# Seven block products instead of eight: the second MLP's first product by 2x2 blocks

## The chip, the cores and the metric

The kernel runs on one core of a Trainium2 chip. Its time is the device time of one execution in microseconds, from three timed executions; beside them one execution was taken by the hardware profiler, with the start and length of each instruction on the five engines: PE (TensorE matmuls; PEld are its weight loads), DVE (VectorE), ACT (ScalarE), POOL (GpSimd), and SP, whose queue issues the DMAs.

## The reference

Attention over pooled keys and values, followed by two MLPs ("layers" here) on the 4608 x 512 result:

```python
k_p = k.reshape(B, H, Sp, pool, D).mean(axis=3)          # B=8, H=8, S=576, D=64, pool=8
v_p = v.reshape(B, H, Sp, pool, D).mean(axis=3)
attn = softmax(scale * q @ k_p.T)                         # maximum subtracted, sum + 1e-9
x = (attn @ v_p) -> 4608 x 512
h = x @ w_in1;  x1 = (h * sigmoid(h)) @ w_out1            # 512 x 2048, 2048 x 512
h = x1 @ w_in2; out = (h * clip(h + 3, 0, 6) / 6) @ w_out2
```

The weights come as 64-bit floats.

## The kernel before, in words

The tokens are cut into 9 groups of 512, and the 2048 hidden columns into 16 chunks of 128 (`f`). The first layer runs group by group, each through its 16 chunks; then the second layer does the same. Each operand is kept as two float32r halves, high and low, and a product is made of three: high x high, low x high, high x low.

For one chunk, `h_mm` (L426) makes 12 matmuls into a PSUM tile `hps` of 512 tokens: 3 products x 4 pieces of the 512 contracted columns, each with a weight load of 128 columns and 512 moving columns. `act_a` and `act_b` turn it into `gh` and `gl`: ACT applies the activation (L439 tanh in the first layer, L444 relu in the second), DVE multiplies (L440, L445), ACT copies the rounded high half (L453), DVE subtracts for the low half (L454). `y_mm` (L471) then makes 12 matmuls of 512 columns into four PSUM tiles `y0` to `y3` that collect a whole group. PE runs `y_mm` of a chunk behind `h_mm` of the next one. When a group is through, `y_out` evacuates y0 and y2 on ACT (L480), y1 and y3 on DVE (L482), and SP writes them out: to DRAM tiles `x1` in the first layer, to the output in the second.

In the first layer the attention for the next group's four tiles of 128 tokens is put between the chunks (`scores` L286, softmax on DVE and ACT, transposes, `weighted` L390, `split_x` L406 and L407). The keys and values of a batch are pooled beside it: `pool_k` (L217, DVE) and `pool_v` (L227 to L229, POOL). Also beside it the second layer's weights are turned from 64-bit to two float32r halves, in half pieces of 256 columns (`half_a` on ACT and DVE, `half_b` on ACT and POOL, L168 and L169), and written to DRAM tiles `w2`. In the last group of the first layer they are loaded back, two of 512 KB per chunk (`load_split`), and the second layer keeps all of them in SBUF. The second layer's x of each group is loaded from `x1` and split on ACT and POOL (L502, L503).

Each engine executes its instructions in the order in which the program has them; there is no scheduler, the loops set that order, and semaphores make an instruction wait for its operands and for the buffers that it overwrites. PSUM has two buffers for `hps`, two for the attention's `aps`, and the four y tiles. At the start `warm_wide` lets PE work on zeros (L263, L265, L267), before any data has come; L274 to L390 are attention of the first tiles.

The functions that the change touches:

Of the kernel before, what the change touches and what calls it, by code (L numbers as in the profile page):

```python
# [9 lines left out]
F32 = mybir.dt.float32  # L10
# [8 lines left out]
POOL = 8  # L19
# [5 lines left out]
def kernel(  # L25
# [25 lines left out]
    PW = 2 * SP  # L51
    Q = 32
# [6 lines left out]
    p2 = ctx.enter_context(tc.tile_pool(name="p2", bufs=2))  # L59
    dram = ctx.enter_context(tc.tile_pool(name="dram", bufs=1, space=DRAM))  # L60
# [35 lines left out]
    def split_a(layer, f, piece, mul=False):  # L96
# [4 lines left out]
        mag = p2.tile([P, DM], F32, tag="wmag", name="wmag", bufs=4)  # L101
# [31 lines left out]
    HW = DM // 2  # L133
# [4 lines left out]
    def load_half(f, piece, a):  # L138
        raw = p2.tile([P, HW, 2], U32, tag="wmag", name="hraw", bufs=4)
# [4 lines left out]
    def half_a(f, piece, a):  # L144
        raw = half_raw[f, piece, a]
        hw = raw[:, :, 1]
        mag = p2.tile([P, HW], F32, tag="hmag", name="hmag", bufs=1)
# [15 lines left out]
    def half_b(f, piece, a):  # L163

        raw = half_raw.pop((f, piece, a))
        mag = half_mag.pop((f, piece, a))
        t = raw.rearrange("p f w -> p (f w)").rearrange("p (a f) -> p a f", a=2).bitcast(F32R)
        nc.scalar.activation(t[:, 0], mag, AF.Copy)  # L168
        nc.gpsimd.tensor_tensor(out=t[:, 1], in0=mag, in1=t[:, 0].bitcast(F32), op=ALU.subtract)  # L169
        later.append(lambda: nc.sync.dma_start(  # L170
            out=w2[f][piece][:, :, a * HW:(a + 1) * HW], in_=t.bitcast(F32)
        ))

    def load_split(f, piece):
        t = wts.tile([P, 2, DM], F32R, tag=f"{'io'[piece]}{f}", name="whl")
        nc.sync.dma_start(out=t.bitcast(F32), in_=w2[f][piece])
        if piece == 0:
            t = t.rearrange("p a (c f) -> p a c f", f=P)
        w_sl[1, f, piece] = (t[:, 0], t[:, 1])
# [16 lines left out]
    def load_v(b, j, tag=None):  # L196
        if tag:
            t = staging(tag, 2 * POOL * D)[:SP]
        else:
            t = p2.tile([SP, 2 * POOL * D], F32, tag="v", name="vraw", bufs=1)  # L200
# [45 lines left out]
    def load_q(t, tag=None):  # L246
        qt = staging(tag, DM) if tag else p2.tile([P, DM], F32, tag="q", name="qT")
# [517 lines left out]
```

## Time and profile before

| | |
|---|---|
| three timed executions | 1667.47, 1669.53, 1669.57 us; median 1669.53 |
| profiled execution | 1669.22 us, span 1667.4 us |
| PE, busy | 1615.8 us, 97% of the span, 8016 matmuls |
| DVE, ACT, POOL, busy | 49%, 34%, 15% of the span |
| mean granted PE clock | 0.99 |
| first chunk of the second layer starts at | 914.9 us |

A row of the order of time gives start, length, engine, line of the kernel, instruction, what it writes and reads by the program's names, and how many equal ones were merged; in brackets the idle time of the engine before it and who ended that. Matmuls are pipelined: a row of eight lasts from the first one's start to the last one's end, while the next row starts before that end. So PE's pace is read from starts.

### The profile page before, as it was taken

To read this page: it belongs to the slowest core of one execution; us is meant where nothing else is said; L and a number is where in the kernel's file an instruction comes from. 1 tells how busy PE (TensorE), PEld (TensorE's weight loads), DVE (VectorE), ACT (ScalarE), POOL (GpSimd) and SP (SyncE) were. 2 spreads that over 40 slices of the span, in tenths; PEclk is the share of its full clock that TensorE was granted. 3 is DMA by queue.
4 is the path that set the end of the run, shared out by engine and by line. 5 is a ranking of instruction groups with operands and counts; after the bars stand their busy time and mean duration, and the time that the engine had idled before them with its cause. 6 is when DMAs were issued, how large, how long until landed. Compare 5 with 4: busy or idle time off the path is not lost.

```text
span 1667.4 us, 20343 instructions
## 1 busy us (share of the span) xinstructions
PE 1615.8 (97%) x8016; PEld 1395.7 (84%) x8016; DVE 820.8 (49%) x1356; ACT 560.6 (34%) x1007; POOL 255.1 (15%) x258
## 2 busy tenths in 40 slices
PE   7777999999999999999999999999999999999999
PEld 6565888888878888888888888888888888888887
DVE  6999768667676676744422222222222222222222
ACT  5354433334333333322222323232323232222322
POOL 4755413022131120300000000000000000000000
PEclk9799999999999999999999999999999999999999
DMA  9250335345353443311156201010101010101000
GB/s 298 90 201 21 120 124 163 116 128 182 124 157 113 159 146 131 128 45 63 40 198 218 82 7 45 7 44 7 45 7 45 7 44 7 44 7 45 1 26 26
DMA packets 77184, 144.33 MB, mean 87 GB/s; under 512 B 7840, under 2 KB 32288, under 8 KB 77088
## 3 DMA queue, kind: packets, MB, share of 16 engines
q1 hardware_dynamic: 77088, 143.03, 26.0%
q8 instruction: 63, 1.03, 0.3%
q14 instruction: 33, 0.27, 0.1%
HBM read 96.34 MB, written 46.66 MB: 86 GB/s over the span
## 4 chain that ended last, share of the span: by engine, by line
PE 84%; DVE 8%; DMA 4%; issue 2%; ACT 1%; SPq 1%; POOL 0%; DVEq 0%; POOLq 0%; ACTq 0%
PE y L471 41%; PE hps L426 40%; PE aps L390 1%; PE aps L286 1%; DVE wmag L109 1%; DVE wmag L106 1%; DVE gl L454 1%; DVE wmag L116 1%; DVE t L440 1%; DMA wraw<-in_moe_w_out_dram 1%; DMA hraw<-in_moe_w_out_dram 1%; DMA stage<-in_v_dram 1%; DMA stage<-in_q_dram 1%; DMA bl<-bT 0%; DMA wraw<-in_moe_w_in_dram 0%
## 5 line engine op out<-in xcount | busy, mean ns | idle before, releaser
L426 PE MATMUL hps<-xh,whl 128*128 128x512 f32 x2304 | 546.4, 380 | 4.2 <-POOL whl L127 2.1
L426 PEld LDWEIGHTS hps<-xh,whl 128*128 128x128 f32 x2304 | 435.9, 189 | 67.4 <-POOL whl L127 2.5
L471 PE MATMUL y<-gh,whl 128*128 128x512 f32 x1152 | 357.4, 392 | 1.6 <-POOL whl L127 1.2
L471 PE MATMUL y<-whl,gh 128*128 128x512 f32 x1152 | 342.6, 379 | 0.0
L454 DVE TENSOR_TENSOR gl<-t,gh 128x512 fp32r<-128x512 f32 x288 | 221.1, 768 | 190.5 <-ACT gh L453 190.5
L445 DVE SCALAR_TENSOR_TENSOR t<-t,hps 128x512 f32<-128x512 f32 x144 | 99.1, 688 | 436.3 <-ACT t L444 436.3
L426 PE MATMUL hps<-xl,whl 128*128 128x512 f32 x1152 | 296.8, 380 | 1.8 <-DVE xl L407 1.8
L453 ACT ACTIVATE gh<-t 128x512 fp32r<-128x512 f32 x288 | 181.3, 630 | 290.8 <-DVE t L440 181.5
L471 PEld LDWEIGHTS y<-gh,whl 128*128 128x128 f32 x1152 | 217.2, 193 | 39.3 <-issue 3.7
L426 PEld LDWEIGHTS hps<-xl,whl 128*128 128x128 f32 x1152 | 218.1, 190 | 34.0 <-DVE xl L407 3.0
L471 PEld LDWEIGHTS y<-whl,gh 128*128 128x128 f32 x1152 | 217.7, 189 | 30.9
L444 ACT ACTIVATE t<-hps,three 128x512 f32<-128x512 f32 x144 | 99.2, 689 | 422.2 <-PE hps L426 422.2
L471 PE MATMUL y<-gl,whl 128*128 128x512 f32 x576 | 223.4, 388 | 13.5 <-DVE gl L454 13.4
L471 PE MATMUL y<-whl,gl 128*128 128x512 f32 x576 | 218.4, 379 | 0.0
L440 DVE SCALAR_TENSOR_TENSOR t<-t,hps 128x512 f32<-128x512 f32 x144 | 97.8, 679 | 164.6 <-ACT t L439 164.0
L439 ACT ACTIVATE t<-hps 128x512 f32<-128x512 f32 x144 | 85.8, 596 | 260.8 <-PE hps L426 260.6
L503 POOL TENSOR_TENSOR xl<-xr,xh 128x512 fp32r<-128x512 f32 x36 | 45.9, 1274 | 826.4 <-ACT xh L502 826.4
L471 PEld LDWEIGHTS y<-gl,whl 128*128 128x128 f32 x576 | 111.2, 193 | 33.3 <-DVE gl L454 17.1
L471 PEld LDWEIGHTS y<-whl,gl 128*128 128x128 f32 x576 | 108.9, 189 | 15.8 <-DVE gl L454 0.3
L169 POOL TENSOR_TENSOR hraw<-hmag,hraw 128x256 fp32r<-128x256 f32 x64 | 47.0, 734 | 387.5 <-ACT hraw L168 343.3
L127 POOL TENSOR_TENSOR whl<-wmag,whl 128x512 fp32r<-128x512 f32 x32 | 53.2, 1681 | 50.1 <-ACT whl L126 50.0
L310 ACT ACTIVATE pr<-pr 128x288 f32<-128x288 f32 x64 | 28.4, 443 | 85.2 <-DVE pr L303 85.2
(76 smaller groups left out, 929.0 us busy)
## 6 DMA issues: line engine op xcount, KB each, us to landing
w<-hraw SPq DMA_DIRECT2D x64, 256.0 KB
whl<-w SPq DMA_DIRECT2D x32, 512.0 KB
bl<-bT SPq DMA_DIRECT2D x28, 384.0 KB
x<-o SPq DMA_DIRECT2D x36, 256.0 KB
xr<-x SPq DMA_DIRECT2D x36, 256.0 KB
out_dram<-o SPq DMA_DIRECT2D x36, 256.0 KB
wraw<-in_moe_w_in_dram SPq DMA_DIRECT2D x16, 512.0 KB
wraw<-in_moe_w_out_dram SPq DMA_DIRECT2D x16, 512.0 KB
```

The lines of the kernel that those rows point to most:

```text
L127: nc.gpsimd.tensor_tensor(out=t[:, 1, :], in0=mag, in1=t[:, 0, :].bitcast(F32), op=ALU.subtract)
L169: nc.gpsimd.tensor_tensor(out=t[:, 1], in0=mag, in1=t[:, 0].bitcast(F32), op=ALU.subtract)
L310: nc.scalar.activation(p_t[t][:, a], p_t[t][:, a], AF.Exp, scale=ESCALE)
L426: nc.tensor.matmul(ps, w[:, c, :], shuffled(x[:, c, :]), start=(c == 0 and n == 0), stop=(c == NKC - 1 and n == 2),)
L439: nc.scalar.activation(t2, h, AF.Tanh, scale=0.5)
L440: nc.vector.scalar_tensor_tensor(out=t2, in0=t2, scalar=1.0, in1=h, op0=ALU.add, op1=ALU.mult)
L444: nc.scalar.activation(t2, h, AF.Relu, bias=three)
L445: nc.vector.scalar_tensor_tensor(out=t2, in0=t2, scalar=6.0, in1=h, op0=ALU.min, op1=ALU.mult)
L453: nc.scalar.activation(gh, t, AF.Copy)
L454: nc.vector.tensor_tensor(out=gl, in0=t, in1=gh.bitcast(F32), op=ALU.subtract)
L471: nc.tensor.matmul(ps, a, shuffled(b), start=(f == 0 and n == 0), stop=(f == NF - 1 and n == 2))
L503: nc.gpsimd.tensor_tensor(out=xl[:, c, :], in0=r, in1=xh[:, c, :].bitcast(F32), op=ALU.subtract)
```

## The change

The second layer's first product, 512 tokens x 512 by 512 x 512 for a round of four chunks (`d` = 0 to 3), is taken as a 2x2 by 2x2 product of blocks of 256, in seven block products (Winograd's form of Strassen's scheme) instead of eight. It takes seven combined blocks of the weights per round (`ws`) and seven combined blocks of x per group (`x_st`), and sums of the products afterwards.

- *Weights.* In groups 1 to 7 of the first layer `pair_jobs` takes two chunks' half pieces, adds and subtracts them on POOL (`combine`), splits each of the seven results into high and low and writes it to `ws`. The second product's weights go to `w2` as before. The steps are spread over 12 of 16 chunks (`SPLITTING`), so that the 81 steps fill nearly seven groups, where 64 filled a good five before.
- *SBUF.* Attention's tiles lie in a pool `att` that is closed before the last group of the first layer; the second layer's new tiles (`late`) take its place. Three of the seven factors per round stay in SBUF (`STAYING`), the other four (`PASSING`) have one buffer each and are loaded again for every round.
- *Operands of x.* `make_x` makes the seven blocks of a group from the four loaded blocks of `x1`: four differences and seven subtracts for the low halves on POOL, seven copies on ACT. For the next group this is done in rounds 2 and 3 of a group, between the halves.
- *A round.* PE makes product 0, 5, a y, 4, 6, a y, 3, 1, a y, 2, a y; the y are those of the round before. Each product is 12 matmuls of 256 columns. A copy on ACT (L878) and seven sums on DVE (L862) make the four quarters u4, u3, c1, u2 of h; `act_half` activates each: relu (L612), multiply (L613, both operands in SBUF), copy (L620), subtract (L621).
- *Keys and values.* They are loaded at every fourth chunk instead of every second and pooled two chunks later, and the buffers of `kraw` go from two to one; the transposed probabilities `bT` share a buffer with `vraw`.

The diff, cut to its core:

```diff
-    def half_b(f, piece, a):
-        raw = half_raw.pop((f, piece, a))
-        mag = half_mag.pop((f, piece, a))
-        t = raw.rearrange("p f w -> p (f w)").rearrange("p (a f) -> p a f", a=2).bitcast(F32R)
+    def half_b(mag, dst):
+        t = p2.tile([P, 2, HW], F32R, tag="o", name="hs", bufs=4)
         nc.scalar.activation(t[:, 0], mag, AF.Copy)
         nc.gpsimd.tensor_tensor(out=t[:, 1], in0=mag, in1=t[:, 0].bitcast(F32), op=ALU.subtract)
...
+        later.append(lambda: nc.sync.dma_start(out=dst, in_=t.bitcast(F32)))
+    def combine(op, out, a, b):
+        nc.gpsimd.tensor_tensor(out=out, in0=a, in1=b, op=op)
...
+    def pair_jobs(p, rest):
+        d, j = divmod(p, 2)
+        f = 2 * p
+        m = half_mag
+        a11, a12, a21, a22 = (f, 0, 0), (f, 0, 1), (f + 1, 0, 0), (f + 1, 0, 1)
+        def out(k, key):
+            return lambda: half_b(m[key], ws[d][k][:, j])
+        def out_w(i, a):
+            return lambda: half_b(m[f + i, 1, a], w2[f + i][:, :, a * HW:(a + 1) * HW])
+        def make(op, to, x, y):
+            return lambda: combine(op, m[to], m[x], m[y])
+        first, second = rest
+        rest[:] = [out_w(1, 0)], [out_w(1, 1)]
+        return [
+            (a22, first),
+            (a21, second + [out(3, a22)]),
+            (a11, [make(ALU.add, a22, a21, a22), out(4, a22)]),
+            (a12, [out(0, a11)]),
+            (None, [make(ALU.subtract, a21, a11, a21), out(6, a21), make(ALU.subtract, a22, a22, a11)]),
+            (None, [out(5, a22), make(ALU.subtract, a22, a12, a22)]),
+            ((f, 1, 0), [out(2, a22)]),
+            ((f, 1, 1), [out(1, a12)]),
+            ((f + 1, 1, 0), [out_w(0, 0)]),
+            ((f + 1, 1, 1), [out_w(0, 1)]),
+        ]
...
+    PASSING = (0, 4, 1, 2)
+    STAYING = (5, 6, 3)
+    w_st = {}
+    def load_factor(d, k):
+        i = PASSING.index(k) if k in PASSING else 4 + 3 * d + STAYING.index(k)
+        t = wts.tile([P, 2, 2, HW], F32R, tag=f"i{i}", name="wst")
+        nc.sync.dma_start(out=t.bitcast(F32), in_=ws[d][k])
+        w_st[d, k] = t
...
+    def load_x1(g):
+        for k in range(2):
+            for n in range(2):
+                r = late["pool"].tile([P, 2, HW], F32, tag="r", name="xr", bufs=4)
+                rows = x1[g][k * HW:(k + 1) * HW, n * HW:(n + 1) * HW]
+                nc.sync.dma_start(out=r, in_=rows.rearrange("(c p) t -> p c t", p=P))
+                x_raw[k, n] = r.rearrange("p c t -> p (c t)")
+    MADE = (0, 4, 5, 6, 1, 3, 2)
+    def make_x(g, i):
+        k = MADE[i]
+        b11, b12, b21, b22 = (x_raw[a, b] for a in range(2) for b in range(2))
+        src = (b11, b11, b11, b12, b21, b21, b22)[i]
+        if i == 1:
+            combine(ALU.subtract, b11, b12, b11)
+        elif i == 2:
+            combine(ALU.subtract, b11, b22, b11)
+        elif i == 3:
+            combine(ALU.subtract, b12, b22, b12)
+        elif i == 5:
+            combine(ALU.subtract, b21, b21, b11)
+        t = late["x"][(7 * g + i) % 9]
+        nc.scalar.activation(t[:, 0], src, AF.Copy)
+        nc.gpsimd.tensor_tensor(out=t[:, 1], in0=src, in1=t[:, 0].bitcast(F32), op=ALU.subtract)
+        x_st[g, k] = t.rearrange("p a (c n) -> p a c n", c=2)
+    def product(bank, g, d, k):
+        pool, tag = bank
+        ps = pool.tile([P, GT], F32, tag=tag, name=f"p{k}")
+        w = w_st[d, k].rearrange("p j a (c f) -> p j a c f", f=P)
+        x = x_st[g, k]
+        for j in range(2):
+            for n, (a, b) in enumerate(((0, 0), (1, 0), (0, 1))):
+                for c in range(2):
+                    nc.tensor.matmul(
+                        ps[:, j * HW:(j + 1) * HW],
+                        w[:, j, a, c, :],
+                        shuffled(x[:, b, c, :]),
+                        start=(j == 0 and n == 0 and c == 0),
+                        stop=(j == 1 and n == 2 and c == 1),
+                    )
+        return ps
...
+    def act_half(h, half, gh, gl):
+        t = p2.tile([P, GT], F32, tag="t", name="t")
+        nc.scalar.activation(t, h, AF.Relu, bias=three)
+        nc.vector.scalar_tensor_tensor(
+            out=t, in0=t, scalar=6.0, in1=h, op0=ALU.min, op1=ALU.mult
+        )
+        t3 = t.rearrange("p (j n a) -> p j a n", j=2, a=2)
+        oh, ol = (
+            x.rearrange("p j (h a n) -> p j h a n", h=2, a=2)[:, :, half] for x in (gh, gl)
+        )
+        nc.scalar.activation(oh, t3, AF.Copy)
+        nc.vector.tensor_tensor(out=ol, in0=t3, in1=oh.bitcast(F32), op=ALU.subtract)
...
+        SPLITTING = (0, 1, 1, 1, 0, 1, 1, 1, 1, 1, 1, 1, 0, 1, 1, 0)
...
-                todo = stages(g) if layer == 0 else [[] for _ in range(NF)]
+                todo = stages(g)
+                if g == NG - 1:
+                    early.close()
+                    open_late()
                 for f in range(NF):
...
                     due = len(done)
                     conv_a(1, 0)
-                    if halves_b:
-                        half_b(*halves_b.pop())
+                    for job in jobs_b:
+                        job()
+                    jobs_b = []
                     act_b(layer, g, f, tt)
-                    if NF <= n < (NG - 1) * NF and f % 4 and halves_in:
-                        halves_b.append(halves_in.pop(0))
-                        half_a(*halves_b[0])
-                    nxt = layer * NG + g + 1 - NG
-                    if 0 <= nxt < NG:
-                        if f % 4 == 0:
-                            load_x1(nxt, f // 4)
-                        elif f % 4 == 2:
-                            split_x1(nxt, f // 4)
+                    if NF <= n < (NG - 1) * NF and SPLITTING[f] and jobs:
+                        key, jobs_b = jobs.pop(0)
+                        if key:
+                            half_a(*key)
+                    if g == NG - 1:
+                        if f == 0:
+                            load_x1(0)
+                        elif f % 2 == 0 and f < 12:
+                            make_x(0, f // 2 - 1)
                     conv_b(due)
                     if 1 in now:
...
                         kv_wait = []
-                        if kv_jobs and TPG * (g + 1) + f // 4 + 3 >= first_tile[kv_jobs[0][0]]:
+                        if kv_jobs and f % 4 == 1 and TPG * (g + 1) + f // 4 + 4 >= first_tile[kv_jobs[0][0]]:
...
-                        load_split(s, 1)
-        y_mm(*pend)
-        y_out(*pend[:2])
+                        if s < 4:
+                            load_factor(0, PASSING[s])
+                        else:
+                            load_factor((s - 4) // 3, STAYING[(s - 4) % 3])
+                        load_split(s)
+        load_factor(NF // 4 - 1, STAYING[2])
...
+        for g in range(NG):
+            for d in range(NF // 4):
+                more = g + 1 < NG
+                nd = (d + 1) % (NF // 4)
+                go = more or d + 1 < NF // 4
+                c1 = p2.tile([P, GT], F32, tag="gh", name="c1")
+                u2 = p2.tile([P, GT], F32, tag="gl", name="u2")
+                u3 = late["pool"].tile([P, GT], F32, tag="u3", name="u3")
+                u4 = late["pool"].tile([P, GT], F32, tag="u4", name="u4", bufs=1)
+                def add(out, a, b):
+                    nc.vector.tensor_tensor(out=out, in0=a, in1=b, op=ALU.add)
+                def passed(k):
+                    if go:
+                        load_factor(nd, k)
+                def made(*items):
+                    for i in items:
+                        make_x(g + 1, i)
+                if g == 0 and d == 0:
+                    open_rest()
+                    make_x(0, 5)
+                    make_x(0, 6)
+                p1 = product((ps_h, "h"), g, d, 0)
+                passed(0)
+                nc.scalar.activation(c1, p1, AF.Copy)
+                add(u2, c1, product((ps_a, "a"), g, d, 5))
+                y_next()
+                if g == 0 and d == 0:
+                    load_split(NF - 1)
+                if more and d == 1:
+                    load_x1(g + 1)
+                if more and d == 2:
+                    made(0)
+                p5 = product((ps_h, "h"), g, d, 4)
+                passed(4)
+                add(u3, u2, product((ps_a, "a"), g, d, 6))
+                add(u4, u3, p5)
+                add(u2, u2, p5)
+                y_next()
+                gh2, gl2 = rows_of("gh2", 1), rows_of("gl2", 1)
+                act_half(u4, 1, gh2, gl2)
+                if more and d == 2:
+                    made(1)
+                if more and d == 3:
+                    made(2, 3)
+                add(u3, u3, product((ps_a, "a"), g, d, 3))
+                act_half(u3, 0, gh2, gl2)
+                add(c1, c1, product((ps_h, "h"), g, d, 1))
+                passed(1)
+                gh1, gl1 = rows_of("gh1", 2), rows_of("gl1", 2)
+                act_half(c1, 0, gh1, gl1)
+                y_next()
+                if more and d == 3:
+                    made(4, 5)
+                add(u2, u2, product((ps_a, "a"), g, d, 2))
+                passed(2)
+                act_half(u2, 1, gh1, gl1)
+                y_next()
+                if more and d == 3:
+                    made(6)
+                for f, gh, gl, j in ((1, gh2, gl2, 0), (3, gh2, gl2, 1), (0, gh1, gl1, 0), (2, gh1, gl1, 1)):
+                    g_t[1, g, 4 * d + f] = (gh[:, j], gl[:, j])
+                    todo.append((1, g, 4 * d + f))
+        while todo:
+            y_next()
```

The order of instructions at three places. PE in the second layer, before: one chunk's first product (`hps`) and one chunk's y.

```order
L426 MATMUL hps<-xh,whl 128x512 x8
L426 MATMUL hps<-xl,whl 128x512 x4
L471 MATMUL y_12293<-whl,gh 128x512 x2
L471 MATMUL y_12293<-whl,gl 128x512
L471 MATMUL y_12294<-whl,gh 128x512 x2
L471 MATMUL y_12294<-whl,gl 128x512
L471 MATMUL y_12295<-whl,gh 128x512 x2
L471 MATMUL y_12295<-whl,gl 128x512
L471 MATMUL y_12296<-whl,gh 128x512 x2
L471 MATMUL y_12296<-whl,gl 128x512
L426 MATMUL hps<-xh,whl 128x512 x8
```

The same place now: the beginning of a round, products 0 and 5 (`p`), a y of the round before, products 4 and 6.

```order
L597 MATMUL p_8237<-xst,wst 128x256 x12
L597 MATMUL p_8253<-xst,wst 128x256 x12
L522 MATMUL y_8267<-whl,gh_8163 128x512 x2
L522 MATMUL y_8267<-whl,gl_8164 128x512
L522 MATMUL y_8268<-whl,gh_8163 128x512 x2
L522 MATMUL y_8268<-whl,gl_8164 128x512
L522 MATMUL y_8269<-whl,gh_8163 128x512 x2
L522 MATMUL y_8269<-whl,gl_8164 128x512
L522 MATMUL y_8270<-whl,gh_8163 128x512 x2
L522 MATMUL y_8270<-whl,gl_8164 128x512
L597 MATMUL p_8291<-xst,wst 128x256 x12
L597 MATMUL p_8306<-xst,wst 128x256 x12
```

Where one product of 12 long matmuls stood between two y, one or two of 12 short ones stand.

ACT in the second layer, before, over five chunks: relu and copy by turns, and a copy of x (`xh`) now and then.

```order
L444 ACTIVATE t<-hps,three 128x512
L453 ACTIVATE gh<-t 128x512
L502 ACTIVATE xh<-xr 128x512
L444 ACTIVATE t<-hps,three 128x512
L453 ACTIVATE gh<-t 128x512
```

ACT now, in the last round of a group, up to the first copy of the next group's first round (`c_8812`): `xst` are the copies for the next group's block operands.

```order
L612 ACTIVATE t<-u_8619,three 128x512
L620 ACTIVATE gh_8705<-t 128x2x256
L584 ACTIVATE xst<-xr 128x512 x2
L612 ACTIVATE t<-u_8618,three 128x512
L620 ACTIVATE gh_8705<-t 128x2x256
L612 ACTIVATE t<-c_8616,three 128x512
L620 ACTIVATE gh_8753<-t 128x2x256
L584 ACTIVATE xst<-xr 128x512 x2
L612 ACTIVATE t<-u_8617,three 128x512
L620 ACTIVATE gh_8753<-t 128x2x256
L584 ACTIVATE xst<-xr 128x512
L878 ACTIVATE c_8812<-p_8816 128x512
```

Five of the seven operand copies of a group now stand among the four halves of its predecessor's last round.

ACT now, at the end of a group's first round: the evacuation of the y tiles (`o`) of the group before.

```order
L620 ACTIVATE gh_8943<-t 128x2x256
L612 ACTIVATE t<-u_8813,three 128x512
L620 ACTIVATE gh_8943<-t 128x2x256
L532 ACTIVATE o<-y_8267 128x512
L532 ACTIVATE o<-y_8269 128x512
L878 ACTIVATE c_9007<-p_9011 128x512
```

The evacuation stands behind the last half of the round, and ahead of the next round's first copy.

## Rows read from the trace of the kernel before

**Rows 1.** The page's part on busy time: us, share of the span, instructions.

```profile
PE 1615.8 (97%) x8016; PEld 1395.7 (84%) x8016; DVE 820.8 (49%) x1356; ACT 560.6 (34%) x1007; POOL 255.1 (15%) x258
```

**Rows 2.** Stretches: us, busy us and instructions by engine, clock, DMA share, GB/s.

```profile
181.00:832.00 651.00, 646.80 (x3434) 556.38 (x3433) 426.75 (x810) 231.61 (x450) 106.00 (x130) 1.00 0.38 123
832.00:915.00 83.00, 83.00 (x386) 72.70 (x385) 23.05 (x34) 22.70 (x38) 5.11 (x4) 1.00 0.60 206
915.00:1661.00 746.00, 746.00 (x3458) 653.24 (x3457) 209.59 (x307) 215.25 (x338) 40.77 (x32) 1.00 0.08 27
```

**Rows 3.** Order of time in the second layer: start, us, engine, line, instruction.

```profile
1640.06 1.89 PE L426 MATMUL hps<-xh,whl 128*128 128x512 f32 x8
...
1642.91 0.69 ACT L444 ACTIVATE t<-hps,three 128x512 f32<-128x512 f32 x1 [3.11 <-PE hps L426]
...
1643.64 0.69 DVE L445 SCALAR_TENSOR_TENSOR t<-t,hps 128x512 f32<-128x512 f32 x1 [3.10 <-ACT t L444]
...
1644.36 0.63 ACT L453 ACTIVATE gh<-t 128x512 fp32r<-128x512 f32 x1 [0.75 <-DVE t L445]
...
1645.02 0.69 DVE L454 TENSOR_TENSOR gl<-t,gh 128x512 fp32r<-128x512 f32 x1 [0.69 <-ACT gh L453]
...
1645.24 1.89 PE L426 MATMUL hps<-xh,whl 128*128 128x512 f32 x8
```

**Rows 4.** Order of time on PE, the first 22 us.

```profile
7.29 1.28 PE L265 MATMUL aps<-probe 128*128 128x256 f32 x10
8.41 2.90 PE L267 MATMUL aps<-probe 128*128 128x512 f32 x10
...
13.83 4.09 PE L286 MATMUL aps<-kbd,stage 128*128 128x144 f32 x32
17.75 1.28 PE L274 MATMUL aps<-ident 128*128 128x128 f32 x10
```

**Rows 5.** Order of time in the first layer, around 396 us.

```profile
395.75 1.27 POOL L227 TENSOR_TENSOR vraw<-vraw 72x512 f32<-72x512 f32 x1 [0.82 <-DMA vraw<-in_v_dram]
...
396.00 1.57 DVE L454 TENSOR_TENSOR gl<-t,gh 128x512 fp32r<-128x512 f32 x1 [0.69 <-ACT gh L453]
```

**Rows 6.** Order of time on ACT, around 408 us.

```profile
408.32 0.63 ACT L453 ACTIVATE gh<-t 128x512 fp32r<-128x512 f32 x1 [1.66 <-DVE t L440]
...
408.85 0.51 ACT L149 ACTIVATE hmag<-hraw 128x256 f32<-128x256 f32 x1
```

**Rows 7.** Groups by line: busy us, mean ns of one, idle before.

```profile
L503 POOL TENSOR_TENSOR xl<-xr,xh 128x512 fp32r<-128x512 f32 x36 | 45.9, 1274 | 826.4 <-ACT xh L502 826.4
...
L502 ACT ACTIVATE xh<-xr 128x512 fp32r<-128x512 f32 x36 | 22.1, 613 | 0.0
...
L407 DVE TENSOR_TENSOR xl<-aps,xh 128x512 fp32r<-128x512 f32 x36 | 24.3, 680 | 0.9 <-ACT xh L406 0.8
...
L439 ACT ACTIVATE t<-hps 128x512 f32<-128x512 f32 x144 | 85.8, 596 | 260.8 <-PE hps L426 260.6
...
L169 POOL TENSOR_TENSOR hraw<-hmag,hraw 128x256 fp32r<-128x256 f32 x64 | 47.0, 734 | 387.5 <-ACT hraw L168 343.3 <-issue 39.8 <-DMA hraw<-in_moe_w_in_dram 4.4
```

**Rows 8.** Order of time on PE, around 127 and 163 us.

```profile
127.00 0.76 PE L286 MATMUL aps<-kbd,qT 128*128 128x144 f32 x4 [2.77 <-DVE xl L407]
...
163.09 0.80 PE L471 MATMUL y<-gl,whl 128*128 128x512 f32 x1 [4.33 <-DVE gl L454]
```

**Rows 9.** Stretches around those two waits.

```profile
98.00:163.00 65.00, 48.18 (x254) 39.95 (x253) 62.80 (x74) 33.39 (x58) 36.19 (x25) 1.00 0.25 91
163.00:167.00 4.00, 3.91 (x10) 3.04 (x10) 3.32 (x9) 1.93 (x4) 0.00 (x0) 0.57 0.18 65
```

**Rows 10.** Order of time around the scores of one tile.

```profile
406.07 1.50 DVE L217 TENSOR_REDUCE kbd<-kraw 64x72 f32<-64x576 f32 x2
...
413.98 0.68 DVE L407 TENSOR_TENSOR xl<-aps,xh 128x512 fp32r<-128x512 f32 x1
...
416.19 1.14 PE L286 MATMUL aps<-kbd,qT 128*128 128x144 f32 x8
```

More of the change, by code (lines that the diff above doesn't have):

```diff
@@ L1 @@
+import functools
 import math
@@ L51 @@
     PW = 2 * SP
+    HW = DM // 2
     Q = 32
@@ L174, in load_split, with w2_jobs @@
[L174 to L179, printed above, removed]
+        later.append(lambda: nc.sync.dma_start(out=dst, in_=t.bitcast(F32)))
+    def combine(op, out, a, b):
+        nc.gpsimd.tensor_tensor(out=out, in0=a, in1=b, op=op)
+    def w2_jobs():
+        rest = [[], []]
+        for p in range(NF // 2):
+            for i, (key, split) in enumerate(pair_jobs(p, rest)):
+                yield key, split
+        yield None, rest[0] + rest[1]
@@ new lines, in load_split @@
+    def load_split(f):
+        t = wts.tile([P, 2, DM], F32R, tag=f"o{f}", name="whl")
+        nc.sync.dma_start(out=t.bitcast(F32), in_=w2[f])
+        w_sl[1, f, 1] = (t[:, 0], t[:, 1])
+    PASSING = (0, 4, 1, 2)
[6 more added lines that the diff above has]
+        w_st[d, k] = t
@@ L199, in load_v @@
         else:
-            t = p2.tile([SP, 2 * POOL * D], F32, tag="v", name="vraw", bufs=1)
+            t = att.tile([P, 2 * POOL * D], F32, tag="v", name="vraw", bufs=1)[:SP]
         nc.sync.dma_start(out=t, in_=v[b, j])
@@ L437, in act_a @@
         t2, h = in_two(t), dealt(ps)
[L438 to L447 removed]
+        nc.scalar.activation(t2, h, AF.Tanh, scale=0.5)
+        nc.vector.scalar_tensor_tensor(
+            out=t2, in0=t2, scalar=1.0, in1=h, op0=ALU.add, op1=ALU.mult
+        )
         return t
@@ L459, in y_mm @@
         oh, ol = w_sl[layer, f, 1]
-        if f == 0:
+        if f == FIRST[layer]:
             y_ps[layer, g] = [
@@ L471, in y_mm @@
                 nc.tensor.matmul(
-                    ps, a, shuffled(b), start=(f == 0 and n == 0), stop=(f == NF - 1 and n == 2)
+                    ps, a, shuffled(b), start=(f == FIRST[layer] and n == 0),
+                    stop=(f == LAST[layer] and n == 2),
                 )
@@ L489, in y_out @@
             nc.sync.dma_start(out=dst, in_=o)
-    x1_t = {}
-    def load_x1(g, c):
-        r = x1_t[g, c] = p2.tile([P, GT], F32, tag="q", name="xr")
-        nc.sync.dma_start(out=r, in_=x1[g][c * P:(c + 1) * P, :])
-    def split_x1(g, c):
-        if c == 0:
-            new_x(NG + g)
-        xh, xl = xs[NG + g]
-        r = x1_t.pop((g, c))
-        nc.scalar.activation(xh[:, c, :], r, AF.Copy)
-        nc.gpsimd.tensor_tensor(out=xl[:, c, :], in0=r, in1=xh[:, c, :].bitcast(F32), op=ALU.subtract)
+    late = {}
@@ new lines, with open_late, open_rest @@
+    x_raw = {}
+    x_st = {}
+    def open_late():
+        pool = late["pool"] = ctx.enter_context(tc.tile_pool(name="late", bufs=2))
+        four = p2.tile([P, 4, 2, GT], F32R, tag="x", name="xst")
+        one = pool.tile([P, 2, GT], F32R, tag="xst", name="xst", bufs=1)
+        late["x"] = [four[:, i] for i in range(4)] + [one]
+    def open_rest():
+        four = p2.tile([P, 4, 2, GT], F32R, tag="x", name="xst")
+        late["x"] += [four[:, i] for i in range(4)]
+    def load_x1(g):
[5 more added lines that the diff above has]
+                x_raw[k, n] = r.rearrange("p c t -> p (c t)")
@@ L700 @@
                         probs_T(now[2])
-                    if n >= 5 and layer == 0 and f % 2 == 1:
+                    if n >= 5 and f % 2 == 1:
                         for b, j in kv_wait:
```

83 lines of the change are left out of this document (41 added, 42 removed).

## The prediction

> **What bounds the kernel now.** I read the page's busy times first, then the stretches, then the order of time. PE is busy for 97% of the span [rows 1]. Cut by stage, it is busy for 646.8 of 651 us in the middle of the first layer and for every microsecond of the last group of that layer and of the second layer, at a granted clock of 1.00, which is the 2.4 GHz level [rows 2]. DVE and ACT are busy there for 28% and 29%, POOL for 5%. So the second layer lasts as long as PE's list of matmuls. From one chunk's first product to the next it takes 1645.24 - 1640.06 = 5.18 us for 24 matmuls of 512 columns [rows 3], 0.2158 us each; a group of 16 chunks takes 82.9 us.
>
> **The profiled execution** took 1669.2 us around a span of 1667.4, 0.3 us under the median of 1669.5, so its sum can be set beside the medians as it is.
>
> **First term: PE's work.** Four chunks' first products were 4 x 12 matmuls of 512 columns, 48 x 0.2158 = 10.36 us. A round of the change has seven block products of 12 matmuls of 256 columns, 84, an eighth fewer columns but 36 more weight loads. The trace has such matmuls: ten of 256 columns, each with its load of 128 columns and the same stride of reading, start at 7.29, and what follows them starts at 8.41 [rows 4]: 0.112 us each. A half of 0.2158 would be 0.108, and the 144-column matmuls on unrounded operands behind them, with loads of the same size, take (17.75 - 13.83)/32 = 0.1225 [rows 4]; these are the bounds, and I take 0.1117, since the probe has the very form. 84 x 0.1117 = 9.38; a round saves 0.975 us, and 36 rounds (9 groups of 4) save **35.1 us** (46 at 0.108, 2.5 at 0.1225). PE's round is then 9.38 + 4 x 2.59 = 19.74 us.
>
> The Trainium skill, page "TensorE: Matmul & The Clock Gate", section "LDWEIGHTS (loading the stationary operand)", sets a load by its columns alone, 128/1.2 GHz or an estimated 107 ns, whatever the moving side is; the section "Back-to-back issue gap" gives 262 cycles, 109 ns, for 256 columns. By the larger of the two the term would be 42.7 us; the probe's 112 ns is above both, so the row decides. What speaks against the change in it is that the load no longer shrinks with the matmul: at 256 columns nothing is left to hide it.
>
> **Second term: the sums, and the wait that they make.** In the kernel before, a chunk needed relu, multiply, copy, subtract: 2.80 us from 1642.91 to 1645.71 on ACT and DVE in turn [rows 3], with 2.4 us to spare. Now each half chunk needs that chain and a sum ahead of it, and the four stand one behind the other in both queues. Per round DVE has 7 sums and 8 other operations, 7 x 0.68 + 8 x 0.69 = 10.3 us [rows 3, 7], ACT 9 operations, 5.9 us. Both fit in 19.74. What matters is the order.
>
> Count from a round's start. PE: products 1.34 and 2.68, y 5.27, products 6.61 and 7.95, y 10.54, products 11.88 and 13.22, y 15.81, product 17.15, y 19.74. The sum with the fourth product starts at about 8.2, the second is done at 9.6, its half at 12.4; three more times (0.68 + 2.80 + 0.03) ends at 22.9, the last ACT copy at 22.2. In a group's first round the y tiles are evacuated after that: ACT takes y0 at 22.1 (it starts an independent operation 0.1 us before the recorded end of the one before [rows 6]) to 22.7, DVE y1 from 22.9 to 23.5. PE wants y0 again at 19.74 + 2.68 = 22.42 and y1 0.65 later. So even a group without any lag waits about 0.45 us there. Before, y's evacuation met idle ACT and DVE.
>
> There is a lag, made in a group's last round by the next group's block operands. ACT's copies of them stand among the halves, and two of these copies wait for a POOL difference that itself stands behind a POOL subtract (1.27 us each [rows 7]). In that round: ACT copy of the third operand 11.6 to 12.2, POOL subtract to 13.5, POOL difference to 14.8, ACT copy of the fourth to 15.5; only now the next half's relu, whose sum was done at 13.1, to 16.1. DVE's multiply reads two SBUF tiles, and such an operation that starts while POOL runs is held until POOL ends: 1.57 us instead of 0.69 [rows 3, 5]. POOL's subtract runs to 16.8, so the multiply ends at 17.5, copy 18.15, subtract 18.9; sum 19.5, relu 20.2, multiply 20.95, copy 21.6, subtract 22.3. The fifth operand's copy ends at 22.1, POOL subtract 23.5, difference 24.75, copy of the sixth 25.4; the last half's relu 26.0 (its sum was done at 23.0), multiply held by POOL to 26.8, then 27.5, copy 28.15, the seventh operand's copy 28.65, and behind it the copy of the new round's first product (0.60 [rows 7]) at 29.15. The second sum of the new round ends at 30.5, which is 10.8 of its own time, where without the lag it is 8.9: 1.9 to 2.0 us late. Everything behind is late by that, y0's evacuation too. PE waits 0.45 + 2.0 = 2.4 us at its y matmul, with the rest of the round queued behind it, in each of the 8 groups after the first: **+19 us** (0.45 x 8 = 4 if the lag is taken up, 4 x 8 = 32 if DVE is held at each of its eight two-tile operations). In the other rounds PE waits for nothing: the first half pair is complete at 15.9, wanted at 22.4.
>
> A wait of that size should not cost the clock: after 2.77 us of idle PE [rows 8] the clock stayed at 1.00, after 4.33 it fell, to 0.57 over 4 us [rows 9].
>
> **Third term: the change of layers, +1 us.** In the first round PE has one y of the first layer left and none of the second, so its list is y 2.59, products 2.68, y 2.59, products 6.70 and, of the next round, 2.68: it wants the first new y at 17.2. The fourth product ends at 10.5, the two sums at 12.2, two halves 2.80 and 3.51 later at 18.5, the copy 0.7 before: a wait of 0.6 to 1.3 us.
>
> **Fourth term: the first layer, +3 us.** The weights' sums add 56 operations on POOL, 32 differences and sums and 24 subtracts (88 where there were 64), 56 x 0.73 = 41 us [rows 7], and 24 ACT copies; POOL's share of the stretch goes from 106 to 147 of 651 us [rows 2]. PE does not wait for POOL there, but DVE is held by it, up to 0.88 us a time [rows 3, 5]. DVE has 224 us of idle time in the stretch, so most of this is covered; without that cover 41 us would be the most. The last pooling of a k block also moves to right ahead of the scores that need it: 1.50 us behind an xl that ends at 414.66, thus 416.2, with scores at 416.19 [rows 10]: nothing, or up to 1 us in six batches. Below zero it can gain the 4.2 us that PE idles now. I take +3, near nothing, with -4 to +12 as ends.
>
> **What costs nothing.** Reloading four of the seven factors each round is 4 x 0.52 MB in 19.74 us, 106 GB/s, where 206 were moved while the second layer's weights were loaded [rows 2]; each has 18.4 us between its last use and its next. SP's queue in the first round has four outputs, held until y3 is evacuated, ahead of these loads, 5 us of the 18. 88 writes of 0.26 MB instead of 64 are 6 MB more over 600 us, beside 123 GB/s moved there now [rows 2]. The next group's operands cost POOL 11 x 1.27 us of 79. The tail is as before: two y chunks, 5.2 us, cover the last half's 3.5.
>
> **Sum:** 1669.2 - 35.1 + 19 + 1 + 3 = 1657.1; I say **1657**.
>
> **Rivals.**
> - *The lag is taken up* (less blocking on ACT than I chain, so that the new group starts on time): the wait is 0.45 us, the sum 1669.2 - 35.1 + 4 + 1 + 3 = 1642. For it: each step in my chain is only some tenths late. Against: five POOL operations stand in it one behind another.
> - *The first layer pays* (slower): POOL's 56 new operations each hold DVE by half of 0.88 us, 25 us, and DVE is what PE waits for. Place: DVE's subtract into gl ahead of y. 1657 - 3 + 25 = 1679; it decides from 12 us more than I take. Against: DVE's idle third.
> - *Weight loads set the pace* (slower): at 0.1225 us a block matmul the round saves 0.07 us; waits shrink, since PE's 144 block matmuls between the lag's start and the y matmul take 1.6 us more: 1669.2 - 2.5 + 7 + 1 + 3 = 1678. It decides from 0.117 us. Against: the probe.
> - *The factors come late*, so the round isn't PE's: each 0.3 us of it costs 11 us. Against: the 206 GB/s.
>
> **How the numbers follow.** My case 0.53 (1649 to 1666), taken-up lag 0.18, first layer 0.14, pace 0.10, late factors 0.05. A measurement tells 0.2%, 3.3 us, from no change. Below 1666.2 lie nearly all of the first two, 0.68; the top of my case and the beginnings of the slower ones give 0.16 within, 0.16 above. From 1642 to 1675 leaves 0.2 out.
>
> **What would show it.** Block matmuls about 0.112 us apart; in each group's second round one PE wait of 2 to 3 us at a y matmul, released by ACT's evacuation of y0; ACT copies of block operands with waits for POOL ahead of them; first layer within some us of 915. Wrong if that wait is missing, if PE waits at products or for factors, or if the first layer grows by over 12 us.

## The result and the profile after

The changed kernel took **1687.70 us** (median of four, 1686.11 to 1689.02), the kernel before 1669.13 beside it (1667.47 to 1669.57): 1.0113 times as long, interval 1.0095 to 1.0130. I had said 1657, with 1642 to 1675 as range: wrong in sign, and outside the range. The profiled execution took 1689.02 us around a span of 1687.2, 19.8 more than that of before.

The busy times and the stretches, which answer to [rows 1, 2]; in the stretches the columns are the length, busy us and instructions by engine, the granted clock, DMA share and GB/s:

```profile
PE 1602.4 (95%) x9312; PEld 1419.0 (84%) x9312; DVE 1031.0 (61%) x1608; ACT 631.8 (37%) x1094; POOL 381.8 (23%) x377
```

```profile
181.00:832.00 651.00, 648.37 (x3440) 558.41 (x3440) 448.70 (x812) 237.55 (x476) 149.23 (x186) 1.00 0.41 132
832.00:915.00 83.00, 83.00 (x386) 72.70 (x385) 23.17 (x34) 22.83 (x39) 11.42 (x9) 1.00 0.61 207
915.00:1661.00 746.00, 709.86 (x4650) 656.28 (x4649) 388.91 (x545) 274.73 (x393) 117.07 (x90) 0.98 0.41 125
```

The first layer is as it was: PE is idle there for 2.6 us instead of 4.2, though POOL works 149 us instead of 106. The second layer, where PE had been busy for every microsecond, now has PE idle for 36 of 746 us, and the mean clock is 0.98. What PE waited for between 940 and 1640 us (total us, times, longest):

```profile
PE y L522 <- ACT o L532: 29.7, 8, 3.7
PE p L597 <- DVE u L862: 5.1, 8, 0.7
```

Two places, each once in each of the eight groups behind the first. The order of time shows both in the first group where they occur (start, us, engine, line, instruction; in brackets the idle time before it and who ended that):

```profile
989.16 2.84 PE L597 MATMUL p<-xst,wst 128*128 128x256 f32 x24
...
993.95 1.27 POOL L178 TENSOR_TENSOR xr<-xr 128x512 f32<-128x512 f32 x1
...
994.43 2.84 PE L597 MATMUL p<-xst,wst 128*128 128x256 f32 x24
995.25 0.63 ACT L584 ACTIVATE xst<-xr 128x512 fp32r<-128x512 f32 x1 [2.84 <-POOL xr L178]
995.79 0.71 ACT L612 ACTIVATE t<-u,three 128x512 f32<-128x512 f32 x1
995.96 1.28 POOL L585 TENSOR_TENSOR xst<-xr,xst 128x512 fp32r<-128x512 f32 x1 [0.74 <-PE p L597]
996.53 1.26 DVE L613 SCALAR_TENSOR_TENSOR t<-t,u 128x512 f32<-128x512 f32 x1 [3.19 <-ACT t L612]
...
997.11 0.60 PE L522 MATMUL y<-whl,gh 128*128 128x512 f32 x2
...
997.82 0.88 ACT L620 ACTIVATE gh<-t 128x512 fp32r<-128x512 f32 x1 [1.32 <-DVE t L613]
...
998.73 0.84 DVE L621 TENSOR_TENSOR gl<-t,gh 128x512 fp32r<-128x512 f32 x1 [0.94 <-ACT gh L620]
...
999.11 0.59 ACT L878 ACTIVATE c<-p 128x512 f32<-128x512 f32 x1
...
999.73 0.69 DVE L862 TENSOR_TENSOR u<-c,p 128x512 f32<-128x512 f32 x1 [0.16 <-ACT c L878]
...
1000.47 2.94 PE L597 MATMUL p<-xst,wst 128*128 128x256 f32 x24 [0.61 <-DVE u L862]
...
1011.43 0.80 ACT L620 ACTIVATE gh<-t 128x512 fp32r<-128x512 f32 x1 [0.76 <-DVE t L613]
...
1012.27 0.70 DVE L621 TENSOR_TENSOR gl<-t,gh 128x512 fp32r<-128x512 f32 x1 [0.87 <-ACT gh L620]
...
1015.14 0.66 ACT L620 ACTIVATE gh<-t 128x512 fp32r<-128x512 f32 x1 [0.76 <-DVE t L613]
...
1015.70 1.07 ACT L532 ACTIVATE o<-y 128x512 f32<-128x512 f32 x2
...
1016.33 0.70 PE L522 MATMUL y<-whl,gh 128*128 128x512 f32 x2 [3.72 <-ACT o L532]
...
1017.17 0.50 PEld L522 LDWEIGHTS y<-whl,gh 128*128 128x128 f32 x2 [0.33 <-DVE o L534]
```

This is the chain of the prediction: the copy of the sixth block operand waits 2.84 us for POOL's difference, the relu stands behind it, POOL's subtract holds the multiply to 1.26 us, the new group's first copy (999.11) and sum (999.73) come late, and PE pays at product 3 (0.61 us) and at the y matmul behind y0's evacuation (3.72 us). What the prediction does not have are the wait at product 3 and the lengths of two steps. The groups by line for the second layer (busy us, mean ns of one) answer to the 0.63 and 0.69 of [rows 3]:

```profile
L620 ACT ACTIVATE gh<-t 128x512 fp32r<-128x512 f32 x143 | 119.2, 833 | 126.8 <-DVE t L613 126.8
L621 DVE TENSOR_TENSOR gl<-t,gh 128x512 fp32r<-128x512 f32 x143 | 112.8, 789 | 130.7 <-ACT gh L620 130.7
```

And the stretches about the long wait show a second price:

```profile
1012.60:1016.30 3.70, 0.02 (x1) 0.00 (x0) 2.13 (x4) 1.88 (x4) 0.00 (x0) 1.00 0.00 0
1016.90:1020.30 3.40, 3.40 (x9) 2.52 (x8) 1.41 (x3) 0.36 (x1) 0.00 (x0) 0.50 0.90 305
1020.30:1098.00 77.70, 77.05 (x519) 71.79 (x517) 40.11 (x56) 28.59 (x40) 14.35 (x11) 1.00 0.40 123
```

PE idles for 3.70 us, then works for 3.40 us at 0.50, the 1.2 GHz level, which costs at most half of that, 1.7 us. Two kernels below have such a fall in some groups only, and there a group with it is 1.5 us longer than its neighbour (83.40 against 81.88 us with sums that deal, 82.98 against 81.48 with the differences early). In the changed kernel it happened behind all eight waits: eight stretches of 3.40 us at half clock lower the mean over 746 us by 1.8%, and it is 0.98. From one group's first copy to the next it is 1084.71 - 999.11 = 85.60 us; the mean of the seven such intervals is 85.47, where PE's own work is 4 x 19.74 = 78.96. The 6.5 us over are 0.9 at product 3 (that round takes 20.66 us instead of 19.74, more than the 0.65 that PE idles), 3.72 at the y, 1.5 of clock, and a rest of 0.4, in which the load waits 0.33 us until DVE has evacuated y1. All in all: -35.1 of PE's work, +52.1 in eight groups, +0.8 ahead of the layer (its first product starts at 915.72, where the layer started at 914.9), and, by difference, +2 in the layer's first group make the 19.8.

### The profile page after: what moved, and what is told of

Read it like the earlier page. It is cut to its first block, busy times and chain, and to the rows that moved or that the text cites. A ratio compares the mean times of both kernels' runs of the same rounds, so it can differ in the third digit from the quotient of the medians.

```text
span 1687.2 us, 24141 instructions
## 1 busy us (share of the span) xinstructions
PE 1602.4 (95%) x9312; PEld 1419.0 (84%) x9312; DVE 1031.0 (61%) x1608; ACT 631.8 (37%) x1094; POOL 381.8 (23%) x377
## 4 chain that ended last, share of the span: by engine, by line
PE 63%; DVE 16%; issue 9%; ACT 7%; DMA 3%; POOL 2%; SPq 0%; ACTq 0%; POOLq 0%; DVEq 0%
PE y L522 32%; PE hps L479 18%; PE p L597 10%; DVE t L613 3%; ACT t L612 3%; ACT gh L620 2%; DVE u L862 2%; DVE gl L621 2%; PE aps L340 1%; PE aps L444 1%; POOL xst L585 1%; DVE wmag L111 1%; DVE wmag L114 1%; POOL xr L178 1%; DVE gl L501 1%
## 5 line engine op out<-in xcount | busy, mean ns | idle before, releaser
L479 PE MATMUL hps<-x,whl 128*128 128x512 f32 x1728 | 400.2, 381 | 4.2 <-POOL whl L132 2.1
L597 PEld LDWEIGHTS p<-xst,wst 128*128 128x128 f32 x3024 | 359.0, 192 | 16.3 <-DVE u L862 9.2
L479 PEld LDWEIGHTS hps<-x,whl 128*128 128x128 f32 x1728 | 328.4, 190 | 52.3 <-POOL whl L132 2.5
L597 PE MATMUL p<-xst,wst 128*128 128x256 f32 x3024 | 361.6, 275 | 5.7 <-DVE u L862 5.7
L585 POOL TENSOR_TENSOR xst<-xr,xst 128x512 fp32r<-128x512 f32 x63 | 83.0, 1317 | 659.5 <-ACT xst L584 653.6
L621 DVE TENSOR_TENSOR gl<-t,gh 128x512 fp32r<-128x512 f32 x144 | 113.6, 789 | 131.6 <-ACT gh L620 131.6
L492 DVE SCALAR_TENSOR_TENSOR t<-t,hps 128x512 f32<-128x512 f32 x144 | 97.7, 678 | 152.3 <-ACT t L491 151.4
L862 DVE TENSOR_TENSOR u<-u,p 128x512 f32<-128x512 f32 x180 | 120.2, 684 | 89.6 <-PE p L597 87.5
L612 ACT ACTIVATE t<-u,three 128x512 f32<-128x512 f32 x108 | 77.8, 720 | 251.0 <-DVE u L862 251.0
L174 POOL TENSOR_TENSOR hs<-hmag,hs 128x256 fp32r<-128x256 f32 x88 | 65.0, 743 | 470.6 <-ACT hs L173 415.0
L620 ACT ACTIVATE gh<-t 128x512 fp32r<-128x512 f32 x144 | 120.0, 833 | 127.6 <-DVE t L613 127.6
L613 DVE SCALAR_TENSOR_TENSOR t<-t,u 128x512 f32<-128x512 f32 x108 | 91.0, 843 | 106.6 <-ACT t L612 106.6
```

Source lines behind the costliest of these rows:

```text
L479: nc.tensor.matmul(ps, w[:, c, :], shuffled(x[:, c, :]), start=(c == 0 and n == 0), stop=(c == NKC - 1 and n == 2),)
L492: nc.vector.scalar_tensor_tensor(out=t2, in0=t2, scalar=1.0, in1=h, op0=ALU.add, op1=ALU.mult)
L585: nc.gpsimd.tensor_tensor(out=t[:, 1], in0=src, in1=t[:, 0].bitcast(F32), op=ALU.subtract)
L597: nc.tensor.matmul(ps[:, j * HW:(j + 1) * HW], w[:, j, a, c, :], shuffled(x[:, b, c, :]), start=(j == 0 and n == 0 and c == 0), stop=(j == ...
L612: nc.scalar.activation(t, h, AF.Relu, bias=three)
L613: nc.vector.scalar_tensor_tensor(out=t, in0=t, scalar=6.0, in1=h, op0=ALU.min, op1=ALU.mult)
```

## The experiments

My theory was that the copy and the subtract are long because they read `t` with a stride of two (`t3`, the columns dealt out again), that this makes the halves late, and that the wait, once that long, costs clock as well. The rivals: POOL's differences make the lag and the lengths don't matter; the place of y's evacuation, behind the last half, is the whole of it; the clock is the main price. The first four kernels are the changed one with one edit each, the others combine edits or take a part of one. The ratios are to the kernel before as measured beside them, 1668.67 us for the first four and 1668.74 for the last four.

**Sums that deal.** The sums and c1's copy read PSUM dealt and write plainly, so that copy and subtract read what lies in a row (`plain` and `dealt2` split a row of 512 into two pieces of 256 and each into `(a n)` or `(n a)`, with `a` = 2):

```diff
-        t3 = t.rearrange("p (j n a) -> p j a n", j=2, a=2)
+        t3 = plain(t)
-  nc.vector.tensor_tensor(out=out, in0=a, in1=b, op=ALU.add)
+  nc.vector.tensor_tensor(out=plain(out), in0=plain(a), in1=dealt2(b), op=ALU.add)
-                nc.scalar.activation(c1, p1, AF.Copy)
+                nc.scalar.activation(plain(c1), dealt2(p1), AF.Copy)
```

> The sums read PSUM with the stride of two and write in the dealt order, so that the copy and the subtract of each half read plainly; nothing else. Theory 1 (the wait of 3.7 us at a group's second y is the chain of ACT and DVE running late, in part because the copy takes 0.83 us and the subtract 0.79 where 0.63 and 0.69 were taken): both fall to 0.63 and 0.69, eight halves between lag and wait save 0.3 us each, the wait falls to about 2 us, the 0.65 us wait at a product goes, the clock stays at 1.00; time about 1687.7 - 8 x (2.4 + 1.8) = 1654. Rival 1 (the lag from POOL alone makes the wait): less than 8 us gained, the clock still falls. Rival 2 (PE is held by factors or their DMA): no change.

Measured: 1660.24 us (1659.63 to 1660.85), 0.9950 [0.9935, 0.9964]. The two steps and what PE waited for in it:

```profile
L627 DVE TENSOR_TENSOR gl<-t,gh 128x512 fp32r<-128x512 f32 x141 | 97.6, 692 | 100.4 <-ACT gh L626 100.4
L626 ACT ACTIVATE gh<-t 128x512 fp32r<-128x512 f32 x140 | 88.3, 631 | 124.7 <-DVE t L619 124.7
```

```profile
PE y L522 <- ACT o L532: 19.6, 8, 2.5
```

The copy is 0.20 us shorter, the subtract 0.10, and the sums, which now read PSUM with the stride, are no longer than before (683 ns, 684 in the changed kernel). The wait is 2.46 us: the prediction had 2.4, the expectation above about 2, and the time is 6 us above that expectation. The wait at product 3 is gone; the clock fell behind one of the eight waits (at 1012.7 us). 27.5 us hang on where one stride lies. Without it in the halves, the kernel takes the predicted time within 3.2 us. The round and the group's first copy, sums and evacuation in it:

```profile
987.04 2.84 PE L597 MATMUL p<-xst,wst 128*128 128x256 f32 x24
...
995.89 0.58 ACT L884 ACTIVATE c<-p 128x512 f32<-128x512 f32 x1
...
996.50 0.69 DVE L868 TENSOR_TENSOR u<-c,p 128x512 f32<-128x512 f32 x1 [0.31 <-ACT c L884]
...
1011.45 1.07 ACT L532 ACTIVATE o<-y 128x512 f32<-128x512 f32 x2
```

**Evacuation first.** `y_out` with its y ahead of the last half instead of behind it:

```diff
                 add(u2, u2, product((ps_a, "a"), g, d, 2))
                 passed(2)
-                act_half(u2, 1, gh1, gl1)
                 y_next()
+                act_half(u2, 1, gh1, gl1)
```

> Only the fourth y of a round, and with it the evacuation of y0 to y3, is put ahead of the last half's activation in ACT's and DVE's queues; PE's order stays. Theory 1 (PE waits because y0's evacuation stands behind the late last half): the wait falls from 3.7 to below 0.7 us (now at y1, behind DVE), the clock stays at 1.00, the 0.65 us wait at a product stays; groups of 80 us instead of 85.4, time about 1645. Rival 2 (factors, DMA): no change. If the chain itself were too long for a round, a wait of the same size would turn up at another y.

Measured: 1653.37 us (1652.53 to 1653.72), 0.9908 [0.9893, 0.9923], 8 us more than expected.

```profile
PE p L597 <- DVE u L862: 5.1, 8, 0.7
PE y L522 <- DVE o L534: 4.3, 8, 0.6
PE y L522 <- ACT o L532: 0.6, 4, 0.2
```

The 3.72 us shrink to 0.15 for y0 and 0.55 for y1, and the clock stays at 1.00. The product's wait stays, since the halves are as late as they were. The expectation had named both waits that are left, but not all that they cost: groups take 81.1 us, 2.1 over PE's own work, though PE idles for only 1.35 us of it.

**No differences.** The four POOL differences of x are left out for the groups behind the first:

```diff
-        if i == 1:
+        if g > 0:
+            pass
+        elif i == 1:
```

> The four POOL differences that make a group's block operands are left out for groups 1 to 8 (the copies and subtracts stay). Theory 1: ACT's operand copies wait for no POOL difference, the lag of some 2 to 2.7 us goes, the wait falls from 3.7 to about 1.6 us, which is what the slow copies alone leave, and the clock stays: about 1650. If strided copies were all, the wait would stay at 3 us or more.

Measured: 1649.14 us (1647.61 to 1649.60), 0.9882 [0.9867, 0.9896]. One wait a group is left, of 1.22 us, where 1.6 was expected; groups take 80.6 us.

```profile
PE y L522 <- ACT o L532: 9.7, 8, 1.2
```

So POOL's differences make the lag, as predicted, but the long steps are left with more than the 0.45 us that I had without a lag.

**Filler.** Sixteen matmuls of 512 columns go into product 4's tile, which that product overwrites. They stand ahead of the first y in the second round of the groups behind the first, so that PE works through the wait:

```diff
+                p5 = ps_h.tile([P, GT], F32, tag="h", name="p4")
+                if g > 0 and d == 1:
+                    for _ in range(16):
+                        nc.tensor.matmul(
+                            p5, w_st[d, 5][:, 0, 0, :P], shuffled(w_sl[1, 0, 1][0]),
+                            start=True, stop=True,
+                        )
-                p5 = product((ps_h, "h"), g, d, 4)
+                product((ps_h, "h"), g, d, 4, p5)
```

> Sixteen matmuls of 512 columns (3.45 us) on data that nothing reads are put where PE waits for y0, in the second round of groups 1 to 8, into a PSUM tile that is overwritten afterwards. Theory 1 (a wait of 3.7 us lowers the clock for 3.4 us, and that costs 1.7 to 1.8 us each time): no idle of over 1 us there, clock 1.00 all through the second layer, time 1687.7 - 8 x 1.75 = 1674. If the clock were not part of the cost: no gain, 1688.

Measured: 1679.68 us (1678.23 to 1681.04), 1.0063 [1.0046, 1.0080], where 1674 was expected. The whole second layer, and the place at 1013 us:

```profile
915.00:1653.00 738.00, 726.90 (x4781) 670.34 (x4780) 390.10 (x546) 276.78 (x393) 117.08 (x90) 1.00 0.40 127
```

```profile
1013.17 3.62 PE L884 MATMUL p<-whl,wst 128*128 128x512 f32 x16
...
1015.94 0.88 ACT L621 ACTIVATE gh<-t 128x512 fp32r<-128x512 f32 x1 [0.76 <-DVE t L614]
...
1017.36 0.70 PE L522 MATMUL y<-whl,gh 128*128 128x512 f32 x2 [0.57 <-ACT o L532]
```

Idle PE turned into busy PE at the same place keeps the clock at 1.00. Fillers and what is left of the wait, 16 x 0.2158 + 0.57 = 4.02 us, are 0.3 us longer than the wait of 3.72 that they cover. A group takes 84.36 us, 1.1 less than 85.47, so a fall was worth some 1.4 us; 8.0 us come back in all. The run also shows where most of the 0.3 us comes from: the copy that took 0.66 us beside an idle PE (1015.14 in the changed kernel) takes 0.88 beside the fillers.

**Both edits.** Sums that deal, and the evacuation first:

> Both edits: the sums deal, and y is evacuated ahead of the last half. Theory 1: the chain saves 0.3 us a half, the evacuation no longer stands behind the late half; what is left is at most 0.3 us at y1, evacuated by DVE. Groups of 79.0 to 79.4 us against PE's own 78.96; time about 1660 - 8 x 2.6 = 1639. If a second wait were hidden behind the first, groups would stay above 80.

Measured: **1635.07 us** (1634.14 to 1635.53), 0.9796 [0.9783, 0.9809]: the fastest of all, 52.6 us under the changed kernel and 33.7 under that of before. That is 4 us less than expected. In its second layer PE waits for nothing behind the first group; a group takes 78.96 us, PE's own work to the hundredth. The stretch from the start of the layer:

```profile
915.00:1606.00 691.00, 690.14 (x4631) 644.46 (x4631) 374.75 (x545) 245.47 (x391) 114.60 (x90) 1.00 0.43 135
```

**Both edits, and differences early.** Two of the differences are made in round 2 instead of among the halves of round 3:

```diff
+                    difference(2)
+                    difference(3)
...
-        elif i == 2:
+        elif i == 2 and g == 0:
...
-        elif i == 3:
+        elif i == 3 and g == 0:
```

> As the one before, and the next group's two differences for its third and fourth operand are made one round earlier on POOL, where it is idle. Theory 1: PE no longer waits in the one before, so this gains nothing beyond 0.3 us a group: 1637 to 1639. If the lag still cost something, up to 8 x 1.3 = 10 us less.

Measured: 1635.98 us (1634.85 to 1636.35), 0.9802 [0.9789, 0.9815]: nothing more, since nothing was left to wait for.

**Differences early, alone.** The edit above without the other two:

> Only the two differences are made one round earlier; copies still read with a stride, y is evacuated behind the last half. Theory 1: ACT waits for one POOL operation less, the lag and the wait fall by 0.7 to 1.3 us, the 0.65 us wait at a product goes, the clock stays at 1.00: about 1687.7 - 8 x (1.3 + 1.75) = 1663. If POOL's place in the queue did not matter: 1688.

Measured: 1660.70 us (1658.80 to 1662.40), 0.9951 [0.9937, 0.9964]. There are eight waits of 1.97 to 2.15 us:

```profile
PE y L522 <- ACT o L532: 16.6, 8, 2.1
```

The expectation had the clock at 1.00 throughout, but it fell behind three of them, of 1.97, 2.08 and 2.15 us, and stayed behind five of 2.00 to 2.15. The stretch behind the one of 2.08 us:

```profile
1013.30:1016.70 3.40, 3.40 (x10) 2.72 (x10) 1.16 (x2) 0.10 (x1) 0.00 (x0) 0.53 1.00 327
```

**Sums that deal, no differences.**

> The sums deal, and the four POOL differences are left out for groups 1 to 8: a group without lag and with plain copies. Theory 1, by the prediction's own chain: 0.45 us of waiting at the y tiles, groups of 79.4 us, about 1642. If something else than lag and slow copies held PE at the group's start, groups would stay above 80.

Measured: 1641.42 us (1640.85 to 1641.97), 0.9836 [0.9822, 0.9849].

```profile
PE y L522 <- ACT o L532: 3.0, 8, 0.4
```

With neither the stride nor the differences, PE waits 0.37 us a group, where I had worked out 0.45 for halves without a lag.

## Why the prediction was wrong

- **First term, right.** Block matmuls start 0.112 us apart (24 from 994.43 on, the y behind them at 997.11), and where PE waits for nothing a group takes 78.96 us. The 35.1 us are there.
- **Second term: the step that failed.** Place, chain and number of the y waits were right; two lengths in the chain were not. I took 0.63 us for the copy and 0.69 for the subtract from [rows 3], operations of the same count of elements that read in a row, though the diff shows that both now read `t3`. They take 0.83 and 0.79. With plain reads the chain runs as predicted: counted from the round's first product, the group's first copy ends at 9.4 us (29.15 - 19.74 = 9.4 predicted) and y0's evacuation starts at 24.4 (22.1 + 2.0 = 24.1 predicted). With the stride they are 10.5 and 26.5. Four halves of the lagged round and four of the next stand ahead of that evacuation: 2.1 us over eight halves are 0.27 a half, near the 0.30 by which copy and subtract are longer. PE has paid 0.9 of them at product 3, a wait that the prediction did not have and named as a sign of being wrong; the rest turns 2.46 us at the y into 3.72. Without POOL's differences the stride moves that wait from 0.37 to 1.22. The trace of before had a warning that I quoted and read for something else: the 256-column copy L149 in [rows 6] takes 0.51 us, and it reads every second 32-bit element of the 64-bit weights. Its group beside that of a plain copy of the same size in the kernel before:

```profile
L149 ACT ACTIVATE hmag<-hraw 128x256 f32<-128x256 f32 x64 | 33.4, 521 | 11.7 <-DMA hraw<-in_moe_w_out_dram 8.4 <-DMA hraw<-in_moe_w_in_dram 3.0
L168 ACT ACTIVATE hraw<-hmag 128x256 fp32r<-128x256 f32 x64 | 26.3, 411 | 9.1 <-DVE hmag L157 8.9
```

If the stride is what tells these two apart, a fifth of the time is the stride's (521 against 411 ns); on four copies of 512 columns that would have been some 0.7 to 0.9 us more.
- **The clock, wrong in the same step.** "A wait of that size should not cost the clock" rested on one wait of 2.77 us [rows 8, 9]. At 3.72 us the clock fell eight times of eight; even at 2.46 it fell once in eight, and at 1.97 to 2.15 three times in eight. One wait that did not pay was no bound, and the trace of before has, early on, a wait of 2.94 us behind which the clock was at 0.50 (PE was less busy around it than in the second layer):

```profile
71.73 0.74 PE L286 MATMUL aps<-kbd,qT 128*64 128x144 f32 x2 [2.94 <-DVE kbd L217]
```

```profile
71.80:75.00 3.20, 3.20 (x8) 2.37 (x9) 3.17 (x4) 1.05 (x2) 2.10 (x3) 0.50 0.33 109
```

- **In numbers:** 19 us were taken, 52 measured: 10 from the longer wait, 7 at product 3, 12 from the clock, 4 from the remaining 0.4 us a group; the other 19 are the wait that was predicted. The plain-read kernel gives back 27.5 of the 33 at once. That it comes within 3.2 us of the prediction is in part luck: its eight groups cost 25 us where 19 were taken (0.4 us a group of rest, and one fall of the clock), and the other terms come to less than the 4 us taken.
- **Third and fourth term, small as predicted.** In the layer's first group PE idles 1.3 us at three places (0.6 to 1.3 predicted), and some 2 us are lost by difference. The layer starts 0.8 us later, where 3 were taken; but the experiments, which have the same first layer, start it between 914.02 and 916.38 us, so terms of this size are not resolved. POOL's share of the middle stretch is 149 us (147 predicted), and PE idles no more there.
- **What was to cost nothing cost nothing:** PE waits for no DMA in the second layer, while 125 GB/s are moved in it.
- **The rivals.** The taken-up lag would have been 1642; with the stride gone and the differences left out it is 1641.4, so that sum was sound and its condition was not met. The first layer did not pay, weight loads did not set the pace, no factor was late. No rival on the slow side was the one that came.

The Trainium skill, page "SBUF — State Buffer", section "Door 1: The DMA port swizzle (why `[64,N]` ≈ `[32,N]`)", says that SBUF has lines of 16 bytes and that two hits in a line are enough for the full rate. A read of every other 32-bit element has two, so by this rule the stride is free. With PE idle the strided copy takes 0.66 us against 0.63, near to that; beside a working PE it takes 0.77 to 0.90, which contradicts the rule, and the measurement decides.

## What to carry to other kernels

Take an operation's length from a row with the same access pattern and the same neighbours at work, not only with the same shape: the profile prints no strides, so the code has to be read for them, and a fixed chain multiplies the difference. Where a reordering of elements is needed, put it where it costs nothing; here that was the read of PSUM in the sums. Before giving up on a change that shortens the bottleneck engine's work but makes it wait, ask which wait ends last and whether the work that ends it has to stand where it stands: one line moved and one stride moved turned +1.1% into -2.0%.

## What the runs showed of the hardware that I had not expected

- A stride of two in an SBUF read of 128x512 32-bit elements costs ACT's copy 0.20 us in the mean (833 against 631 ns) and DVE's subtract 0.10 (789 against 692); in a PSUM read it costs DVE's sum and ACT's copy nothing (683 against 684, 584 against 586).
- The copy's price hangs on PE. In the changed kernel the 135 strided copies of the second layer beside which PE works all the time take 0.77 to 0.90 us, and the eight with PE idle (one at 1015.14) 0.66. The filler run puts work on PE at these eight places, and there the copies take 0.87 to 0.89. A plain copy takes 0.63 either way. What in PE's work delays the read stays open.
- Waits near 2 us can lower the clock and need not: three of eight at 1.97 to 2.15 us, one of eight at 2.46, none in the wait of 2.77 us [rows 8]. Their length alone does not tell them apart, since the shortest of these eight was among the three; what does stays open.
